# Where the low bits of a 64-bit weight are made, and when the second weight is converted

## The chip, the cores and the metric

One core of one Trainium2 chip runs the whole program. The metric is the time of one execution on the device in microseconds: 1229.4 us, the median of three runs (1228.87 to 1230.52). The program is scheduled when it is built: the order of the instructions on each engine and of the transfers on each queue is fixed then, from priorities and a model of the times; on the chip each engine works through its own list in order and waits at semaphores.

## The reference

```python
# q, k, v: (4, 8, 576, 64); rotary embedding of q and k, then softmax attention
attn = softmax((q_rot @ k_rot.T) / 8)          # 576 x 576 for each of 32 heads
x = (attn @ v), transposed to (2304, 512)
# layer 1: w_in (512, 2048), w_out (2048, 512)
h = x @ w_in;  r = maximum(h, 0);  x = (s * r * r + b) @ w_out
# layer 2: its own w_in (512, 2048), w_out (2048, 512)
h = x @ w_in;  g = h / (1 + exp(-1.702 * h));  out = g @ w_out     # (2304, 512)
```

The four weights arrive as 64-bit floating-point numbers, everything else as 32-bit.

## The kernel before

**Attention** runs over 144 score tiles of 128 queries by 576 keys, 36 for each of four batches (`bounds` is 0, 36, 72, 108, 144). The program is written in *slots*, one for each score tile: `at(slot, fn, ...)` puts a piece of work into a slot, and the slots' pieces are written out in order, each with a priority that falls from slot to slot. For a tile TensorE makes the scores (`score_tile`), VectorE takes the row minimum of the negated scores (L421), ScalarE the exponential (L431), GpSimd scales by the reciprocal sum (L442), and two slots later TensorE transposes the tile (`turn_tile`), ScalarE casts it to 16 bits (L463) and VectorE makes the rest (L465). `weighted` multiplies with the values at the end of each unit of 4 or 5 tiles and stores to `xT`.

**Layer 1** runs beside attention from slot 42 on, in passes over 256 tokens and 16 blocks of its 2048 inner columns. `target` spreads its half blocks evenly over the slots up to 146, so a slot carries the same amount of TensorE work of layer 1 whenever it runs. What is left of it, and layer 2, follow after attention, when `late` is set: attention's pools are closed (`widen`, in the code after the last slot), and new pools take over their space, with the buffers for layer 2's weights (`fill`, L671 and L558) and for x of layer 1's last pass (L791).

**The weights' conversion** from 64 to 32 bits is done on the chip. A 64-bit number is read as two 32-bit words, high and low. ScalarE scales the high word, read as a float, by 2^-112 (L526, L614), which puts the exponent right; VectorE shifts the low word right by 29, so that three bits are left (L528, L615); VectorE then puts the sign into the low word (L531, L616), and shifts the high word left by 3 and joins the low one (L537, L619). `to_f32` does this for 128x512 numbers at a time. Layer 1's 32 such pieces (`weight`) come during attention, 16 in slots 2 to 34 and 16 in slots 36 to 68, by `conv_slot`; the 16 pieces of layer 2's second weight (`outer_make`) come after attention through the same function.

Layer 2's **first weight** goes through `top_load` and `top_max`, 32 pieces of 128x256: a load into the one buffer `top`, the conversion, the piece's largest absolute value (L622) and a store to `w2f` in DRAM. Before, piece i is loaded in slot 40 + 3i and converted in slot 42 + 3i, so from 40 to 135. `top_send` (137) reduces the maxima and sends them through DRAM (`tops`) to all partitions (`wrow`); `top_scale` (141) makes the scales from them. `combine` reads `w2f` and the scales after attention.

`hold` ties an operation behind the row minimum of the newest score tile in its engine's order while attention runs. Nearly all transfers are issued by SyncE, in one order; an issue that has to wait holds up those behind it.

Of the kernel before, what the change touches and what calls it, by code (L numbers as in the profile page):

```python
# [14 lines left out]
AF = mybir.ActivationFunctionType  # L15
ALU = mybir.AluOpType
# [12 lines left out]
def kernel(  # L29
# [14 lines left out]
    nc = tc.nc  # L44
# [41 lines left out]
    def pin(ins, chain="pe"):  # L86
        if chain in chains:
            tc.add_manual_dep(
                ins.ins,
                chains[chain],  # L90
                mybir.DependencyInfo(
                    mybir.DependencyClass.NoSync, mybir.DependencyReason.SCHED_ONLY
                ),
                reason=chain,
            )
        chains[chain] = ins.ins.name
# [9 lines left out]
    def hold(ins):  # L106
        if anchor and not late:
            tc.add_manual_dep(
                ins.ins,
                anchor[-1],  # L110
                mybir.DependencyInfo(
                    mybir.DependencyClass.NoSync, mybir.DependencyReason.SCHED_ONLY
                ),
                reason="hold",
            )
        return ins

    def f32(ap):
        return ap.bitcast(F32)
# [387 lines left out]
    def dv(ins):  # L507
        if late:
            pin(ins, "dve")
        return ins  # L510

    def pace(ins):
        if "dve" in chains:
            tc.add_manual_dep(
                ins.ins,
                chains["dve"],
                mybir.DependencyInfo(
                    mybir.DependencyClass.NoSync, mybir.DependencyReason.SCHED_ONLY
                ),
                reason="pace",  # L520
            )

    def to_f32(raw):
        words = raw.bitcast(U32).rearrange("p (n z) -> p n z", z=2)
        low, high = words[:, :, 0], words[:, :, 1]
        ins = nc.scalar.activation(f32(high), f32(high), AF.Copy, scale=2.0**-112)  # L526
        pace(hold(ins))
        dv(hold(nc.vector.tensor_scalar(low, low, 29, None, op0=ALU.logical_shift_right)))  # L528
        yield 0.55
        dv(  # L530
            nc.vector.scalar_tensor_tensor(  # L531
                low, high, 0x80000000, low, op0=ALU.bitwise_and, op1=ALU.bitwise_or
            )
        )
        yield 0.75
        dv(
            nc.vector.scalar_tensor_tensor(  # L537
                low, high, 3, low, op0=ALU.logical_shift_left, op1=ALU.bitwise_or
            )
        )  # L540
        yield 0.8
        return f32(low), f32(high)
# [29 lines left out]
    def weight(f, m):  # L572
        if f in STREAMED:
            weight_load(f, m)
            t = wpool.tile([128, 2, 512], F32R, tag=f"ws{m}", name=f"w0_{f}{m}")
        elif f == NF - 1:
            t = wpool.tile([128, 2, 512], F32R, tag=f"w10{1 - m}", name=f"w0_{f}{m}")
            kept.setdefault(f, []).append(t)
        elif m == 0:
            t = wpool.tile([128, 4, 512], F32R, tag=f"w{HELD.index(f)}", name=f"w0_{f}")  # L580
            kept[f] = [t[:, 0:2], t[:, 2:4]]
        if f not in STREAMED:
            t = kept[f][m]
        low, high = at_once(to_f32(halves0.pop((f, m))))
        nc.scalar.copy(t[:, 0], low)
        nc.vector.tensor_tensor(t[:, 1], low, f32(t[:, 0]), op=ALU.subtract)
        if f in STREAMED:
            d = dram.tile([128, 2, 512], F32, tag=f"wd{f}{m}", name=f"wd{f}{m}")
            spill[f, m] = d
            at(conv_slot(f, m) + SPILL, lambda: nc.sync.dma_start(d, f32(t)))  # L590
# [18 lines left out]
    def top_max(i):  # L609
        t = wtop.pop(i)  # L610
        words = t.bitcast(U32).rearrange("p (n z) -> p n z", z=2)
        low, high = words[:, :, 0], words[:, :, 1]
        flat = t.bitcast(F32)[:, 0:256]
        hold(nc.scalar.activation(f32(high), f32(high), AF.Copy, scale=2.0**-112))  # L614
        hold(nc.vector.tensor_scalar(low, low, 29, None, op0=ALU.logical_shift_right))  # L615
        nc.vector.scalar_tensor_tensor(  # L616
            low, high, 0x80000000, low, op0=ALU.bitwise_and, op1=ALU.bitwise_or
        )
        nc.vector.scalar_tensor_tensor(  # L619
            flat.bitcast(U32), high, 3, low, op0=ALU.logical_shift_left, op1=ALU.bitwise_or  # L620
        )
        nc.vector.tensor_reduce(  # L622
            wmax[:, i : i + 1], flat, axis=AX.X, op=ALU.max, apply_absolute_value=True
        )
        nc.sync.dma_start(
            w2f.rearrange("(p c) f -> p (c f)", p=128)[:, i * 256 : (i + 1) * 256], flat
        )
# [88 lines left out]
    def outer_make(f, tag):  # L716
        o = late["m2"].tile([128, 2, 512], F32R, tag="g", name=f"wm{f}", bufs=3)
        low, high = yield from to_f32(take())
        pace(nc.scalar.copy(o[:, 0], low))
        dv(nc.vector.tensor_tensor(o[:, 1], low, f32(o[:, 0]), op=ALU.subtract))  # L720
        yield 0.7
        done_with(1)
        nc.sync.dma_start(made[f], f32(o))
# [24 lines left out]
    late = {}  # L748
# [435 lines left out]
    def at(slot, fn, *args):  # L1184
        tasks.setdefault(slot, []).append((fn, args))
# [120 lines left out]
                at(first - 4, value_load, b, p, vts[p])  # L1306
                at(first - 2, value_split, b, p, vts[p])
    for i in range(32):
        at(40 + 3 * i, top_load, i)
        at(42 + 3 * i, top_max, i)  # L1310
    at(137, top_send)
    at(141, top_scale)
    at(3, v_first, 0, first_scale)
    at(4, v_spread, 0, first_scale)
    for f in range(NF):
# [114 lines left out]
```

## Time and profile before

| what | before |
|---|---|
| median of three runs | 1229.4 us |
| the profiled execution's own time | 1225.09 us |
| its span, first to last instruction | 1222.9 us |
| mean granted TensorE clock | 0.965 |
| bytes read from HBM and written to it | 150.24 MB, 51.12 MB |
| attention's last store | issued at 681.5 us |

The profile is one execution. The span is shorter than the execution's time by what lies around the first and the last instruction. Busy time of an engine leaves out its waits and the issuing of transfers. A granted clock of 1 is TensorE's upper level, 2.4 GHz; in the stretches at 0.5 it ran at the lower one, 1.2 GHz, so a mean of 0.95 says that a tenth of the stretch was at the lower one. The stages, by the starts of the score tiles: tiles 0 to 35 from 26 to 172 us, 36 to 41 to 194 us, 42 to 66 to 322 us, and the last one, tile 143, at 669.6 us.

### The profile page before, as it was taken

The numbers are of one execution on the slowest core, as the hardware profiler recorded it, in microseconds if no ns is written. First come the engines' busy times: TensorE is split into PE (matmuls) and PEld (weight loads), VectorE is DVE, ScalarE is ACT, GpSimd is POOL, SyncE is SP. The second block draws the span as 40 slices with busy tenths as digits, with TensorE's granted clock in tenths as the row PEclk, the third lists the DMA queues.
The fourth block names the chain that finished last, engine by engine and source line by source line (L and its number), as shares of the span: only waits on it lengthen the run. The fifth ranks groups of instructions, "written<-read, shape, count | busy, mean of one in ns | idle before, by whom it ended". The sixth has DMA issues, their size and how long they took to land.

```text
span 1222.9 us, 22833 instructions
## 1 busy us (share of the span) xinstructions
PE 1100.4 (90%) x8160; PEld 941.4 (77%) x8160; DVE 864.2 (71%) x2006; ACT 690.7 (56%) x1477; POOL 266.7 (22%) x295
## 2 busy tenths in 40 slices
PE   3675767989999999999999799989999999999997
PEld 2554546888889999999999698767777777777775
DVE  5877787989978797777776376766665655755544
ACT  2775675756655655566665587876343343443443
POOL 4475753346334343411111000000000000000000
PEclk9877787999999999999999999989999999999999
DMA  6687868899978878776652599834011101010010
GB/s 151 207 231 207 252 193 268 255 311 292 307 223 290 261 239 250 231 228 212 211 187 94 197 364 372 309 109 155 3 35 35 38 1 37 18 35 3 1 35 18
DMA packets 147873, 209.95 MB, mean 172 GB/s; under 512 B 33712, under 2 KB 106672, under 8 KB 147760
## 3 DMA queue, kind: packets, MB, share of 16 engines
q1 hardware_dynamic: 146896, 207.90, 53.6%
q8 instruction: 65, 1.06, 0.4%
q10 hardware_dynamic: 864, 0.59, 0.2%
q14 instruction: 48, 0.39, 0.1%
HBM read 150.24 MB, written 51.12 MB: 165 GB/s over the span
## 4 chain that ended last, share of the span: by engine, by line
PE 61%; DVE 18%; DMA 8%; ACT 6%; issue 5%; POOL 1%; SPq 1%; ACTq 0%; DVEq 0%; POOLq 0%
PE acc L99 26%; PE l L99 22%; PE av L99 4%; PE s L99 4%; PE t L99 4%; DVE P L421 3%; DVE pt L465 2%; PE r L102 1%; DMA w2f<-top 1%; DVE stage L531 1%; DMA top<-in_moe_w_in_dram 1%; DVE stage L528 1%; DVE stage L537 1%; DMA stage<-in_moe_w_out_dram 1%; ACT P L431 1%
## 5 line engine op out<-in xcount | busy, mean ns | idle before, releaser
L99 PE MATMUL acc<-wo,g 128*128 128x512 f32 x864 | 248.6, 413 | 1.3 <-ACT g L949 0.7
L99 PE MATMUL l<-xc,wc 128*128 128x256 f16 (+1 forms) x1680 | 199.2, 263 | 0.7 <-DVE c L942 0.7
L442 POOL TENSOR_SCALAR P<-P,st 128x576 f32<-128x576 f32 x144 | 118.2, 821 | 355.6 <-DVE st L441 185.7
L99 PEld LDWEIGHTS <-wc 128*128 128x128 f16 x1680 | 137.6, 98 | 65.9 <-issue 54.1
L99 PE MATMUL acc<-g,w 128*128 128x256 f32 (+1 forms) x1056 | 162.1, 302 | 10.8 <-DVE g L845 9.9
L99 PEld LDWEIGHTS acc<-wo,g 128*128 128x128 f32 x864 | 148.3, 189 | 26.8 <-ACT g L949 2.5
L99 PEld LDWEIGHTS acc<-g,w 128*128 128x128 f32 x1056 | 141.8, 192 | 18.9 <-DVE g L845 12.2
L431 ACT ACTIVATE P<-P,st 128x576 f32<-128x576 f32 x144 | 112.0, 778 | 66.7 <-DVE P L421 66.4
L421 DVE TENSOR_SCALAR_CACHE_REDUCE P<-s 128x576 f32<-128x576 f32 x144 | 108.1, 750 | 41.0 <-PE s L99 39.2
L99 PE MATMUL t<-ident,P 128*128 128x128 f32 x720 | 111.1, 289 | 26.6 <-POOL P L442 8.8
L99 PE MATMUL l<-xh,w 128*128 128x256 f32 x616 | 126.9, 289 | 7.0 <-ACT r L832 3.1
L99 PEld LDWEIGHTS t<-ident,P 128*128 128x128 f32 x720 | 86.5, 149 | 35.4 <-issue 18.0
L465 DVE TENSOR_TENSOR pt<-t,pt 128x640 f16<-128x640 f32 x120 | 98.2, 818 | 19.2 <-ACT pt L463 17.2
L99 PEld LDWEIGHTS l<-xh,w 128*128 128x128 f32 x616 | 102.0, 193 | 8.5 <-ACT r L832 3.4
L463 ACT CAST pt<-t 128x640 f16<-128x640 f32 x144 | 98.7, 685 | 16.6 <-PE t L99 13.3
L947 ACT ACTIVATE r<-c 128x512 f32<-128x512 f32 (+1 forms) x80 | 46.9, 587 | 105.3 <-DVE c L942 105.3
L99 PE MATMUL l<-xl,w 128*128 128x256 f32 x308 | 87.7, 285 | 3.1 <-DVE xl L800 3.1
L99 PE MATMUL s<-k,qb 128*128 128x320 f32 x480 | 85.6, 304 | 3.4 <-DVE pt L465 2.2
L953 DVE TENSOR_TENSOR g<-c,g 128x512 fp32r<-128x512 f32 (+1 forms) x80 | 51.1, 639 | 45.2 <-ACT g L949 45.2
L832 ACT ACTIVATE r<-l 128x256 f32<-128x256 f32 x144 | 53.3, 378 | 45.8 <-PE l L99 38.1
L99 PEld LDWEIGHTS s<-k,qb 128*128 128x128 f32 x480 | 70.8, 189 | 10.6 <-issue 4.0
L942 DVE SCALAR_TENSOR_TENSOR c<-l,xm,u 128x256 f32<-128x256 f32 (+1 forms) x120 | 54.6, 455 | 33.1 <-PE l L99 29.0
(143 smaller groups left out, 1982.2 us busy)
## 6 DMA issues: line engine op xcount, KB each, us to landing
ws<-wd SPq DMA_DIRECT2D x80, 512.0 KB, 5.4
k<-ksp SPq DMA_DIRECT2D x24, 576.0 KB, 6.2
stage<-in_moe_w_in_dram SPq DMA_DIRECT2D x16, 512.0 KB, 5.4
stage<-in_moe_w_out_dram SPq DMA_DIRECT2D x16, 512.0 KB, 6.1
top<-in_moe_w_in_dram SPq DMA_DIRECT2D x32, 256.0 KB, 3.3
rawTrue<-in_moe_w_out_dram SPq DMA_DIRECT2D x16, 512.0 KB, 6.2
wod<-wm SPq DMA_DIRECT2D x16, 512.0 KB, 7.6
wo<-wod SPq DMA_DIRECT2D x16, 512.0 KB, 4.5
```

What stands on the lines that cost most here:

```text
L99: pin(nc.tensor.matmul(*args, **kw))
L102: pin(nc.tensor.transpose(*args))
L421: ins = nc.vector.tensor_scalar(pr, ps[:, 192 : 192 + S], -Q_SCALE, None, op0=ALU.mult, op1=ALU.min, accum_out=st[:, 0:1],)
L431: nc.scalar.activation(pr, pr, AF.Exp, bias=st[:, 0:1], scale=-1.0, accum_out=st[:, 1:2])
L442: pin(nc.gpsimd.tensor_scalar(pr, pr, st[:, 2:3], 1.0, op0=ALU.mult, op1=ALU.mult), "pool")
L463: nc.scalar.copy(hi, pc)
L465: nc.vector.tensor_tensor(lo, pc, hi, op=ALU.subtract)
L528: dv(hold(nc.vector.tensor_scalar(low, low, 29, None, op0=ALU.logical_shift_right)))
L832: nc.scalar.activation(r, ps[:, cols], AF.Relu)
L942: dv(nc.vector.scalar_tensor_tensor(o, ps, d, rest, op0=ALU.mult, op1=ALU.add))
L947: nc.scalar.activation(r, c, AF.Tanh, scale=0.851)
L953: dv(nc.vector.tensor_tensor(g2[:, 1], c, f32(g2[:, 0]), op=ALU.subtract))
```

## The change

There are two edits. First, during attention ScalarE makes the three low bits, as `low` times 0.984375 x 2^-29 less 0.484375, written back as an unsigned number, which the conversion rounds; VectorE's shift stays in `to_f32` for the 16 pieces after attention alone. Second, piece i of layer 2's first weight is loaded in slot 64 + floor(5i/2) and converted two slots later: loads from slot 64 to 141, two and three slots apart in turn, conversions from 66 to 143; `top_send` goes to slot 145 and `top_scale` to 148.

```diff
+    def eighths(low):
+        hold(nc.scalar.activation(low, low, AF.Copy, bias=-0.484375, scale=0.984375 * 2.0**-29))
+
     def to_f32(raw):
...
-        dv(hold(nc.vector.tensor_scalar(low, low, 29, None, op0=ALU.logical_shift_right)))
+        if late:
+            dv(hold(nc.vector.tensor_scalar(low, low, 29, None, op0=ALU.logical_shift_right)))
+        else:
+            eighths(low)
...
     def top_max(i):
...
-        hold(nc.vector.tensor_scalar(low, low, 29, None, op0=ALU.logical_shift_right))
+        eighths(low)
...
     for i in range(32):
-        at(40 + 3 * i, top_load, i)
-        at(42 + 3 * i, top_max, i)
-    at(137, top_send)
-    at(141, top_scale)
+        at(64 + 5 * i // 2, top_load, i)
+        at(64 + 2 + 5 * i // 2, top_max, i)
+    at(64 + 4 + 5 * 31 // 2, top_send)
+    at(64 + 7 + 5 * 31 // 2, top_scale)
```

## Rows read from the trace of the kernel before

**Rows 1.** The page: busy us, share of the span and instructions of each engine.
```profile
PE 1100.4 (90%) x8160; PEld 941.4 (77%) x8160; DVE 864.2 (71%) x2006; ACT 690.7 (56%) x1477; POOL 266.7 (22%) x295
```
**Rows 2.** Busy time by stretch: us, each engine's busy us (count), clock, DMA share, GB/s.
```profile
26.00:172.00 146.00, 100.27 (x653) 77.50 (x654) 116.44 (x280) 99.05 (x202) 89.26 (x91) 0.80 0.73 210
172.00:194.00 22.00, 13.53 (x90) 9.80 (x88) 15.70 (x43) 14.22 (x30) 4.30 (x7) 0.84 0.87 271
194.00:322.00 128.00, 113.34 (x964) 107.12 (x965) 118.06 (x278) 83.66 (x179) 54.57 (x52) 0.95 0.88 284
322.00:461.00 139.00, 132.28 (x1167) 125.86 (x1166) 115.97 (x290) 82.88 (x187) 56.66 (x62) 1.00 0.82 259
461.00:633.00 172.00, 168.68 (x1498) 163.41 (x1497) 128.96 (x340) 106.91 (x236) 42.88 (x53) 1.00 0.73 229
633.00:681.00 48.00, 46.31 (x414) 43.68 (x412) 28.94 (x79) 23.86 (x52) 6.74 (x9) 1.00 0.27 97
681.00:702.00 21.00, 14.33 (x109) 13.33 (x109) 7.83 (x18) 14.11 (x31) 0.00 (x0) 1.00 0.69 232
```
**Rows 3.** The same of line L421 alone, two records a score tile.
```profile
194.00:322.00 128.00, 18.22 (x49) 0.95 0.88 284
322.00:461.00 139.00, 22.51 (x60) 1.00 0.82 259
461.00:633.00 172.00, 29.69 (x78) 1.00 0.73 229
```
**Rows 4.** The same of tile top: VectorE's and ScalarE's part.
```profile
194.00:322.00 128.00, 14.80 (x32) 3.60 (x8) 0.95 0.88 284
322.00:461.00 139.00, 17.34 (x40) 4.38 (x10) 1.00 0.82 259
461.00:633.00 172.00, 20.81 (x52) 5.82 (x14) 1.00 0.73 229
```
**Rows 5.** The same of line L528, the shift of layer 1's conversion.
```profile
26.00:172.00 146.00, 10.14 (x16) 0.80 0.73 210
172.00:194.00 22.00, 1.43 (x3) 0.84 0.87 271
194.00:322.00 128.00, 6.14 (x12) 0.95 0.88 284
```
**Rows 6.** Tile stage: duration ns min/median/max, first and last start us, shapes.
```profile
L526 ACT ACTIVATE stage<-stage x32: 654/676/721, 44.9 to 320.2; 128x512 f32<-128x512 f32 x32
```
**Rows 7.** Chain of waits by line, 26 to 172 us.
```profile
by line: issue 13.3%; DVE P L421 8.3%; PE av L99 8.3%; PE s L99 5.9%; PE r L102 5.6%; DVE stage L531 5.0%; POOL nat L285 4.8%; DMA stage<-in_moe_w_out_dram 4.3%; DVE stage L528 4.1%; DVE stage L537 3.9%; PE t L99 3.8%; POOL nat L282 3.1%; D
```
**Rows 8.** Tile top, the same columns.
```profile
L614 ACT ACTIVATE top<-top x32: 422/439/466, 194.2 to 632.9; 128x256 f32<-128x256 f32 x32
L615 DVE TENSOR_SCALAR top<-top x32: 272/295/1474, 194.6 to 634.1; 128x256 uint32<-128x256 uint32 x32
L616 DVE SCALAR_TENSOR_TENSOR top<-top x32: 394/423/1244, 197.7 to 634.7; 128x256 uint32<-128x256 uint32 x32
```
**Rows 9.** Line L606, loads of top: from issue to landing.
```profile
DMA to landing us min/median/max: 2.6/3.3/7.3
```
**Rows 10.** Line L625, stores of top: from issue to landing.
```profile
DMA to landing us min/median/max: 1.7/3.7/8.3
```
**Rows 11.** ScalarE's waits, 322 to 633 us: us in total, times, longest.
```profile
ACT top L614 <- DMA top<-in_moe_w_in_dram: 17.3, 6, 4.3
```
**Rows 12.** SyncE's queue, waits of 190 to 690 us, the same columns.
```profile
SPq L606 <- DMA w2f<-top: 61.0, 24, 6.1
...
SPq L671 <- DMA xT<-pt: 3.7, 1, 3.7
```
**Rows 13.** Timeline of SyncE, 635 to 646 us: start us, us.
```profile
636.89 0.32 SPq L630 DMA_DIRECT2D tops<-wscale  x1
644.30 0.32 SPq L631 DMA_DIRECT2D wrow<-tops  x1
```
**Rows 14.** Timeline of SyncE, 681 to 688 us.
```profile
685.66 0.37 SPq L671 DMA_DIRECT2D rawFalse<-w2f  x1
```

## The prediction, made before the result was known

> **What bounds the kernel now.** I read the totals first, then the engines by stretch, then the pace of the score tiles, then the waits. TensorE is busy 90% of the span and VectorE 71% [rows 1], but these are averages over stages with different limits, so the windows decide [rows 2]. From 322 us until the end of attention at 681 us TensorE is the bound: 132.28 of 139 us, 168.68 of 172, 46.31 of 48, all at full clock, while VectorE falls from 83% to 60%. From 194 to 322 us it is another stage: TensorE 113.34 of 128 us (14.7 us idle) at a granted clock of 0.95, and VectorE 118.06 of 128, 92%. There VectorE is the busiest engine, because this stretch carries the second half of layer 1's weight conversion, the first conversions of layer 2's weight and layer 1's own work together. From 26 to 172 us nothing is full: VectorE 80%, ScalarE 68%, TensorE 69% at a clock of 0.80. The pace says the same: each score tile leaves two records at L421, so 49, 60 and 78 records [rows 3] are 24.5 tiles in 128 us (5.22 us each), 30 in 139 (4.63) and 39 in 172 (4.41). A tile carries the same share of layer 1 from slot 42 on, so the first of these stretches loses some 0.6 us a tile to something else than TensorE's work.
>
> **The change part by part.** The sum is made on the profiled execution, 1225.1 us (span 1222.9); the median of the three runs is 1229.4, so 4.3 us are added at the end.
>
> *A, 194 to 322 us (slots 42 to 66).* Eight conversions of layer 2's weight leave, with 14.80 us of VectorE and 3.60 of ScalarE [rows 4] and their loads and stores; conversion 0 now comes at slot 66. Twelve shifts of layer 1's conversion leave VectorE too: 6.14 us [rows 5]. VectorE then has 118.06 - 14.80 - 6.14 = 97.1 us of work. ScalarE gets twelve operations. The trace has none with uint32 on ScalarE; the nearest row is the Copy of the same 128x512 strided half, 0.676 us [rows 6]. Ends: the shift's own 0.42 us if integers were quicker, twice 0.676 if they took two passes; I take 0.676, since tile and strides are the same. ScalarE: 83.66 - 3.60 + 12 x 0.676 = 88.2 us, no bound. At the busy shares of the next stretch (TensorE 0.952, VectorE 0.834) the work would take 113.3 / 0.952 = 119.1 us by TensorE and 97.1 / 0.834 = 116.4 by VectorE. The longer one holds: 8.9 us less, and about 1 us for the part of the low clock level that goes with the idle time. I take -10. Ends: 0, if the stage hangs on transfers (DMA share 0.88) or on latencies, and -21, which is both all the VectorE time taken out (20.9) and all that TensorE idles (14.7) or loses to the clock (0.05 x 128 = 6.4).
>
> *B, 26 to 194 us (slots 0 to 42).* 16 + 3 shifts leave VectorE, 10.14 + 1.43 us [rows 5]; 19 x 0.676 = 12.8 us come to ScalarE, which goes from 113 to 126 of 168. No engine is full, so only what lies on the chain counts: the chain of waits has the shift with 4.1% of 146 us, 6.0 us [rows 7]. Against it, the first combining operation (L531), which waited for one ScalarE operation, now waits for two: up to 16 x 0.676 = 10.8 us if nothing covers it. Behind it in VectorE's queue stand the score minima (L421), for which ScalarE's Exp waits. The cover is VectorE's other work, 80% of the stretch. Ends -7.4 (6.0 and all of the 1.43) and +4.8 (10.8 - 6.0); I take -2.5, near the middle, leaning to the gain because VectorE is the busier of the two.
>
> *C, 322 to 681 us (slots 66 to 143).* Here stood 24 conversions, three slots apart; now all 32 stand here, two and three slots apart in turn. VectorE: about 41 us before (17.34 for ten, 20.81 for thirteen, [rows 4], and one more at 1.6); after, 32 at about 1.66 - 0.30 (the shift, [rows 8]) = 43 us: no difference. ScalarE gains 32 x 2 x 0.439 - 24 x 0.439 = 17.6 us over 359, from 60 to 64%. TensorE hides both. What isn't hidden for sure is the ring: there is one buffer, so load i+1 waits for the landing of store i, and a conversion waits for its load. At the medians, load 3.3, two ScalarE operations 0.88, two VectorE operations 0.85, store 3.7 [rows 8 to 10] make 8.7 us. Two slots at 4.41 are 8.8 us, 2.5 slots 11.0: it just fits, and landings reach 7.3 and 8.3 us. When it doesn't fit, ScalarE stands in front of the late load with the next tile's Exp, relu and cast behind it. Even at three slots ScalarE waited so 6 times, 17.3 us [rows 11], and SyncE 61.0 us for stores with all other loads behind it [rows 12]. TensorE idled 10.0 us in the same 311 us [rows 2], at most 0.58 of ScalarE's wait. If half of the 16 two-slot rounds wait 2.9 us (17.3 / 6), that is 23.2 us, 5.9 more than now, and 0.58 of it is +3.4. I take +3; ends -1 (the waits don't grow) and +17 (worked out under the rivals).
>
> The Trainium skill (DMA: Bandwidth & Descriptors, on the fixed cost of a transfer) gives a transfer about 2.0 us of setup and completion. By that a round would be an estimated 2.0 + 0.88 + 0.85 + 2.0 = 5.7 us, the ring would never wait, and C would be 0 and the sum 3 us lower. The landings here, 3.3 and 3.7 us at the median beside a DMA share of 0.73 to 0.82, are longer, and I go by them.
>
> *D, the end of attention.* The last load moves from slot 133 to 141, the maximum's way through DRAM from 137 to 145, the scales from 141 to 148, after the last tile (143). Before, nothing waited for them: `tops` was issued at 636.89 and `wrow`, when that had landed, at 644.30 [rows 13]. Now the last conversion comes beside tile 143, some 35 us later than beside tile 135 (8 tiles at 4.41): `tops` near 672 on the old clock, `wrow` near 679.5, landed 3.7 to 8.3 us later by the stores' row [rows 10], at 683 to 688, and then reduced. The late buffers take over attention's space, and their first load (L671) waited 3.7 us for attention's last store to land [rows 12] and went out at 685.66 [rows 14]. As far as that wait covers all of attention's tiles, it now ends where it did or, with both transfers slow, near 690. Behind it on SyncE stand the loads of x for layer 1's last pass. TensorE has little left to cover it: 14.33 of 21 us busy from 681 to 702 [rows 2]. I take +1, ends 0 and +5. The last four conversions add 5.4 us of VectorE to a stretch where it is busy 28.94 of 48: hidden.
>
> Sum: -10 - 2.5 + 3 + 1 = -8.5; 1225.1 - 8.5 = 1216.6 us, and 1220.9 on the scale of the median.
>
> **The rivals.**
> 1. *The stage isn't VectorE's.* For it: DMA share 0.88, and VectorE's 92% holds operations stretched beyond their quiet length (6.14 us for twelve shifts of 0.42). Against it: TensorE's share rises exactly where VectorE's falls. Then A is -3 or less, B nothing, C and D stay: 1225.1 - 3 + 3 + 1, about 1230 on the median's scale.
> 2. *The ring sets the pace (slower).* Place: ScalarE and SyncE between slots 66 and 143. All 16 two-slot rounds wait 2.9 us, 46.4 us in place of 17.3; at 0.58 of it TensorE loses 17. It decides from the point where a round lasts more than 8.8 us at the median, 0.1 above my figure. For it: the medians leave nothing over, and the added ScalarE operation lengthens each round. Against: waits of 3 to 4 us late in the stage left no TensorE idle time worth the name (3.3 us in 461 to 633). Sum -10 - 2.5 + 17 + 1 = +5.5: 1234.9.
> 3. *More is freed than counted.* With idle time gone the clock stays at its full level through slots 36 to 66, and the first stretch loses the whole shift: A -15, B -6, C +1, D +1: -19, 1210.4.
> That the conversion isn't moved at all can't be: no data sets the order.
>
> **How the numbers follow.** A difference under 0.2% (2.5 us) can't be told from no change here, so faster begins below 1226.9. Forecast 0.57 (A between -6 and -14: 1216 to 1226), rival 1 0.15, rival 2 0.18, rival 3 0.10. Faster: the forecast, rival 3 and a little of rival 1, 0.70. Same: the rest of rival 1 and the mildest of rival 2, 0.12 and 0.01. Slower: the rest of rival 2, 0.17. For 8 in 10 the range takes the forecast, most of rival 3 and rival 1 and all but the far side of rival 2: 1209 to 1235; the forecast's own range is 1216 to 1226.
>
> **What would show it.** Right: in the stretch from tile 42 to tile 66 TensorE's share rises to about 0.95 and the time falls from 128 to about 118 us; VectorE's busy time there falls to about 97; the 32 early shifts are gone and ScalarE has 32 new operations of about 0.68 us and 32 of about 0.44; the pace of tiles after 66 stays within 0.05 us of 4.63 and 4.41. C is wrong if ScalarE's wait for `top` loads passes 40 us and TensorE's idle time after tile 66 grows by over 8 us. D is wrong if the first late load goes out more than 5 us after attention's last store has landed. The whole prediction is wrong if the stretch from tile 42 to 66 keeps its 5.2 us a tile with VectorE at 80%.

## The result and the profile after

The change makes the kernel slower: 1238.35 us, median of four runs (1236.55 to 1242.82), against 1229.13 (1228.64 to 1230.52) before, a ratio of 1.0074 with a 95% interval of 1.0046 to 1.0103. The forecast was 1220.9, the range 1209 to 1235. The profiled execution took 1236.55 us (before 1225.09), its span is 1234.7 (1222.9).

The engines' totals answer to [rows 1] (PE is TensorE, PEld its weight loads, DVE VectorE, ACT ScalarE, POOL GpSimd, SPq SyncE's queue of transfers):

```profile
PE 1104.6 (89%) x8160; PEld 945.1 (77%) x8160; DVE 848.6 (69%) x1942; ACT 715.0 (58%) x1541; POOL 266.2 (22%) x295
```

VectorE has 64 instructions fewer and ScalarE 64 more, as the diff says. The new operations, tile by tile (duration ns min/median/max, first and last start):

```profile
L524 ACT ACTIVATE stage<-stage x32: 649/661/702, 45.8 to 322.4; 128x512 uint32<-128x512 uint32 x32
...
L524 ACT ACTIVATE top<-top x32: 412/426/448, 321.5 to 671.0; 128x256 uint32<-128x256 uint32 x32
```

They cost what the prediction took from the float Copy beside them (0.676 and 0.439, [rows 6, 8]). The stretches, cut at the starts of the same score tiles as in [rows 2], with attention's end cut once more (us, then the busy time of PE, PEld, DVE, ACT and POOL, granted clock, DMA share, GB/s):

```profile
26.00:174.00 148.00, 99.68 (x653) 76.60 (x654) 116.54 (x264) 107.44 (x219) 92.90 (x91) 0.83 0.76 208
174.00:196.00 22.00, 13.67 (x89) 10.56 (x88) 14.54 (x38) 14.87 (x31) 3.15 (x5) 0.80 0.85 259
196.00:322.50 126.50, 114.25 (x967) 107.87 (x966) 103.90 (x235) 87.11 (x186) 51.47 (x52) 0.93 0.82 265
322.50:460.00 137.50, 132.17 (x1172) 126.45 (x1171) 113.05 (x285) 87.21 (x202) 56.62 (x62) 1.00 0.84 266
460.00:635.00 175.00, 169.07 (x1492) 162.90 (x1492) 128.94 (x335) 111.80 (x253) 43.01 (x53) 1.00 0.72 228
635.00:681.00 46.00, 44.55 (x390) 42.24 (x389) 29.56 (x78) 26.37 (x59) 6.73 (x9) 1.00 0.52 123
681.00:694.00 13.00, 3.62 (x25) 2.67 (x24) 2.13 (x9) 0.41 (x1) 0.00 (x0) 0.63 0.33 67
```

Two things are to be seen. From 196 to 322.5 us, tiles 42 to 66, VectorE's busy time fell from 118.06 to 103.90 us, but the stretch only from 128 to 126.5: the gain that was forecast there did not come. And from 681 to 694 TensorE works 3.62 of 13 us, a hole that the kernel before does not have (14.33 of 21 from 681 to 702). Tile 143 starts at 671.7 us, 2.2 after before; the loads of x go out 10.6 after, of the 11.8 us by which the span grew. So most of the loss in this pair of traces lies in the last 26 us of attention. The timeline there (start, duration, engine, line, in brackets the idle time ahead of it and what ended it):

```profile
674.38 0.81 DVE L465 TENSOR_TENSOR pt<-t,pt 128x640 f16<-128x640 f32 x1
...
674.49 0.32 SPq L636 DMA_DIRECT2D tops<-wscale  x1
...
677.77 0.82 DVE L465 TENSOR_TENSOR pt<-t,pt 128x640 f16<-128x640 f32 x1 [0.31 <-ACT pt L463]
...
682.89 0.32 SPq L637 DMA_DIRECT2D wrow<-tops  x1
...
687.64 0.28 DVE L640 TENSOR_REDUCE wscale<-wrow 128x1 f32<-128x128 f32 x1 [9.05 <-DMA wrow<-tops]
687.85 0.47 DVE L844 SCALAR_TENSOR_TENSOR g<-r,sb,g 128x256 fp32r<-128x256 f32 x1
...
689.06 0.81 DVE L465 TENSOR_TENSOR pt<-t,pt 128x640 f16<-128x640 f32 x1
689.93 3.62 PE L99 MATMUL av<-pt,vf 128*64 128x320 f16 x25 [9.21 <-DVE pt L465]
...
694.14 0.32 SPq L501 DMA_DIRECT2D xT<-pt  x1
...
696.28 0.37 SPq L677 DMA_DIRECT2D rawFalse<-w2f  x1
...
697.72 0.98 SPq L797 DMA_DIRECT2D x<-xT  x2
```

VectorE's list has the reduction of `wrow` (L640) in front of the last tile's rest (L465). `wrow` lands only at 687.6, so VectorE stands for 9.05 us, and with it TensorE, which needs that rest for attention's last product. Those 25 matmuls then take 3.62 us, partly at the lower clock level, where the kernel before has:

```profile
678.95 1.93 PE L99 MATMUL av<-pt,vf 128*64 128x320 f16 x25 [0.40 <-DVE pt L465]
```

The first late load (L677) answers to [rows 14]: 696.28 against 685.66.

The ring's waits answer to [rows 11, 12]. ScalarE's for loads of `top`, 322 to 635 us (us in total, times, longest):

```profile
ACT top L620 <- DMA top<-in_moe_w_in_dram: 22.3, 10, 3.4
```

SyncE's for the store ahead of the next load, 322 to 640 us, in the same columns:

```profile
SPq L612 <- DMA w2f<-top: 49.1, 23, 5.6
```

A new wait stands behind the first, in VectorE's list from 322.5 to 635 us: VectorE no longer waits for the load itself (9.4 us in 5 waits before, 322 to 670 us) but for ScalarE's low bits.

```profile
DVE top L622 <- ACT top L524: 19.1, 13, 2.7
```

### The profile page after: what moved, and what is told of

Read it like the earlier page. It is cut to its first block, busy times and chain, and to the rows that moved or that the text cites. A ratio compares the mean times of both kernels' runs of the same rounds, so it can differ in the third digit from the quotient of the medians.

```text
span 1234.7 us, 22816 instructions
## 1 busy us (share of the span) xinstructions
PE 1104.6 (89%) x8160; PEld 945.1 (77%) x8160; DVE 848.6 (69%) x1942; ACT 715.0 (58%) x1541; POOL 266.2 (22%) x295
## 4 chain that ended last, share of the span: by engine, by line
PE 60%; DMA 14%; DVE 12%; ACT 6%; issue 4%; POOL 2%; SPq 1%; DVEq 0%; ACTq 0%; POOLq 0%
PE acc L99 26%; PE l L99 23%; PE s L99 4%; PE av L99 4%; PE t L99 3%; DMA top<-in_moe_w_in_dram 3%; DVE P L421 2%; DMA w2f<-top 2%; DMA stage<-in_moe_w_in_dram 1%; DVE pt L465 1%; ACT P L431 1%; DMA nat<-in_k_dram 1%; PE r L102 1%; DMA qb<-qsp 1%; DVE wc L704 1%
## 5 line engine op out<-in xcount | busy, mean ns | idle before, releaser
L99 PE MATMUL acc<-g,w 128*128 128x256 f32 (+1 forms) x1056 | 162.9, 303 | 11.3 <-DVE g L851 10.6
L99 PEld LDWEIGHTS acc<-wo,g 128*128 128x128 f32 x864 | 148.3, 189 | 26.8 <-ACT g L955 2.5
L421 DVE TENSOR_SCALAR_CACHE_REDUCE P<-s 128x576 f32<-128x576 f32 x144 | 108.0, 750 | 44.7 <-PE s L99 38.0
L465 DVE TENSOR_TENSOR pt<-t,pt 128x640 f16<-128x640 f32 x120 | 98.2, 819 | 16.7 <-ACT pt L463 14.8
L102 PE MATMUL r<-ident,nat 128*128 128x128 f32 (+1 forms) x160 | 35.1, 327 | 49.4 <-DVE z L307 16.7
```

What stands on the lines that cost most here:

```text
L99: pin(nc.tensor.matmul(*args, **kw))
L102: pin(nc.tensor.transpose(*args))
L421: ins = nc.vector.tensor_scalar(pr, ps[:, 192 : 192 + S], -Q_SCALE, None, op0=ALU.mult, op1=ALU.min, accum_out=st[:, 0:1],)
L465: nc.vector.tensor_tensor(lo, pc, hi, op=ALU.subtract)
```

## The experiments

Ratios are to the kernel before, run on the same chip, with 95% intervals. "66 to 143" is the time between the starts of these tiles, "tail" that from the start of tile 143 to the first late load, both of one profiled execution.

| kernel | median us | ratio | 66 to 143 | tail |
|---|---|---|---|---|
| before | 1229.13 | 1 | 347.8 | 16.1 |
| the change | 1238.35 | 1.0074 [1.0046, 1.0103] | 349.3 | 24.5 |
| tail tied | 1234.8 | 1.0040 [1.0018, 1.0063] | 351.0 | 17.9 |
| slots only | 1243.1 | 1.0097 [1.0065, 1.0129] | 359.4 | 24.7 |
| low bits only | 1231.28 | 0.9994 [0.9974, 1.0014] | 354.0 | 15.8 |
| start 56 | 1253.47 | 1.0178 [1.0148, 1.0208] | 367.1 | 15.9 |
| three slots from 48 | 1228.77 | 0.9976 [0.9955, 0.9996] | 341.7 | 19.4 |
| conversion one slot later | 1241.62 | 1.0103 [1.0068, 1.0139] | 357.6 | 18.1 |
| start 60 | 1251.83 | 1.0167 [1.0146, 1.0189] | 371.7 | 14.1 |
| shorter round | 1230.99 | 0.9999 [0.9980, 1.0018] | 346.0 | 18.5 |
| late tail on before | 1229.88 | 0.9995 [0.9976, 1.0015] | 349.9 | 13.8 |
| three slots from 44 | 1230.58 | 1.0011 [0.9988, 1.0034] | 344.6 | 16.1 |
| three slots from 46 | 1229.45 | 0.9989 [0.9971, 1.0007] | 351.2 | 15.5 |
| own store buffer, 64 | 1229.82 | 1.0004 [0.9985, 1.0022] | 345.9 | 18.9 |
| own store buffer, 60 | 1229.88 | 0.9996 [0.9973, 1.0019] | 347.8 | 13.9 |
| own store buffer, 48 | 1231.51 | 1.0027 [1.0007, 1.0047] | 346.2 | 18.7 |

On one chip 29 runs of the kernel before spread from 1223.9 to 1237.6 us, so a difference of a few us between two single profiles proves nothing; the profiled execution of the store buffer from 64, for one, is the fastest of its twelve (1222.61). The verdicts below go by ratios and by waits that can be pointed at. By the traces TensorE runs the same 8160 operations in the same order in all sixteen kernels; what differs is the lists of the other engines and of the transfers.

**1. The tail tied.** The reduction of `wrow` is put behind the last tile's rest in VectorE's list; only these rows of VectorE's list change places, no other engine's list does.

```diff
-            nc.vector.tensor_tensor(lo, pc, hi, op=ALU.subtract)
+            last_rest.append(nc.vector.tensor_tensor(lo, pc, hi, op=ALU.subtract).ins.name)
...
     def top_scale():
-        up, neg, down = (wscale[:, i : i + 1] for i in range(3))
+        up, neg, down, _ = (*(wscale[:, i : i + 1] for i in range(3)), anchor.append(last_rest[-1]))
```

> The changed kernel with one edge more in the build: the reduction of `wrow` (L640) is put behind the last tile's rest (L465) on VectorE; nothing else moves on any engine. Theory T (VectorE waits 9.0 us for `wrow` in front of the last tile's L465 and L844, and that is the loss): about 9 us faster than the changed kernel, 1229 to 1232 us, and TensorE's gap of 9.2 us before the last av gone. Rival R (the denser ring of loads and stores between slots 66 and 143 costs the time, the wait at the end only shows it): 1236 us or more. Rival W (the late buffers wait for `wrow` all the same, so its reduction is late wherever it stands): about half comes back, 1233 to 1236.

VectorE now finishes the last tile first, and waits for `wrow` with nothing behind it:

```profile
682.52 0.82 DVE L465 TENSOR_TENSOR pt<-t,pt 128x640 f16<-128x640 f32 x1 [1.25 <-ACT pt L463]
...
683.40 1.93 PE L99 MATMUL av<-pt,vf 128*64 128x320 f16 x25 [0.40 <-DVE pt L465]
...
684.85 0.32 SPq L637 DMA_DIRECT2D wrow<-tops  x1
...
690.08 0.29 DVE L640 TENSOR_REDUCE wscale<-wrow 128x1 f32<-128x128 f32 x1 [6.74 <-DMA wrow<-tops]
...
691.90 0.37 SPq L677 DMA_DIRECT2D rawFalse<-w2f  x1
```

The tail goes from 24.5 to 17.9 us: 6.7 of the 8.5 us that the change added come back. The other 1.8 are not the wait for the scales, which were done at 691.32. The first late load went out when attention's last store had landed, at 691.72:

```profile
SPq L677 <- DMA xT<-pt: 5.5, 1, 5.5
```

That store took 5.8 us to land, 4.0 before; the scales alone would have held the load only 0.4 us less. By the medians the step is smaller, from 1.0074 to 1.0040, some 4 us, with intervals that meet. What is left, 0.4% or 5 us, is for the most part not the tail.

**2 and 3. Each half of the change alone.** One has the later slots and VectorE's shift, the other the slots of before and ScalarE's low bits.

The first, against the change (in both conversions):

```diff
-        eighths(low)
+        hold(nc.vector.tensor_scalar(low, low, 29, None, op0=ALU.logical_shift_right))
```

> The later slots alone: the low three bits stay VectorE's shift everywhere. T: the wait for `wrow` is there as in the changed kernel, 1236 to 1241 us. R: also slow, 1236 to 1241, with the time lost between tiles 66 and 143. My sum's part A, if right, shows in tiles 42 to 66: 14.8 us of VectorE gone, 128 us falls to about 121.

The second, with `top_max`, `top_send` and `top_scale` back at 42 + 3i, 137 and 141:

```diff
-        at(64 + 5 * i // 2, top_load, i)
+        at(40 + 3 * i, top_load, i)
```

> ScalarE's three bits alone: loads and conversions of layer 2's weight stay in slots 40 to 135. T: no wait at the end, 1227 to 1231 us. My sum: part of A (6.1 us of VectorE) and B, -2.5 to -6, so 1223 to 1227. A rival, that the added ScalarE operation lengthens each conversion and nothing else was bound by VectorE: 1230 to 1233.

The low bits on ScalarE change nothing clear of noise (0.9994), and the slots alone cost as much as the whole change (1.0097 against 1.0074; the intervals overlap). So the loss belongs to the slots. Tiles 42 to 66 took 121.3 us with the slots alone, as I had expected from part A, and 123.9 with the low bits alone; VectorE was busy for 106.7 and 108.8 us there, and for 103.9 in the change, which took 126.0. So VectorE's load there does not decide. What the slots alone won there went again behind it: tiles 66 to 143 took 359.4 us, 11.6 more than before.

**4. Start at 56.**

```diff
-        at(64 + 5 * i // 2, top_load, i)
-        at(64 + 2 + 5 * i // 2, top_max, i)
-    at(64 + 4 + 5 * 31 // 2, top_send)
-    at(64 + 7 + 5 * 31 // 2, top_scale)
+        at(56 + 5 * i // 2, top_load, i)
+        at(56 + 2 + 5 * i // 2, top_max, i)
+    at(56 + 4 + 5 * 31 // 2, top_send)
+    at(56 + 7 + 5 * 31 // 2, top_scale)
```

> The changed kernel with 56 in place of 64: the same density of the ring (two and three slots apart) and the same ScalarE operation, eight slots earlier, so the last conversion stands in slot 135 and `wrow` is back long before the last tile. T: the loss at the end is gone, 1226 to 1231 us. R: the ring is as dense, so 1236 or more stays.

The tail was cured (15.9 us), but tiles 66 to 143 took 19 us longer than before. Rival R, the dense ring, had said 1236 or more; my theory had not seen it coming. The next four runs ask why.

**5. Three slots a round, from 48**, with the tie and ScalarE's low bits.

```diff
-        at(64 + 5 * i // 2, top_load, i)
-        at(64 + 2 + 5 * i // 2, top_max, i)
+        at(48 + 3 * i, top_load, i)
+        at(50 + 3 * i, top_max, i)
```

> The first experiment (after, with wrow's reduction tied behind the last tile) with one thing more changed: piece i of layer 2's first weight is loaded in slot 48 + 3i and converted in slot 50 + 3i, so every round of the ring has three slots as before the change, and the last conversion stays at slot 143. Theory (the 2.5-slot ring costs about 6 us between tiles 84 and 120): those 36 tiles take 162 us, as before the change (161.7; 168.2 in the first experiment); the gain of tiles 66 to 84 (82.3 against 85.4) goes away as conversions spread; total 1229 to 1233. Rival (any move of the slots reshuffles the order of loads and of TensorE's work, and density is not what costs): tiles 84 to 120 stay at 166 us or more, total 1234 to 1240. A third view, from the run that began at slot 56: conversions of both weights together between slots 48 and 68 cost by themselves; then tiles 48 to 68 lose 3 us or more against before.

Tiles 84 to 120 took 161.4 us, as the ring's theory said (before 161.7), though tiles 66 to 84 kept their gain, which it had not said. Tiles 48 to 68 took 104.3 us against 101.6, a little under the 3 us of the third view. The total, 0.9976, lies just under no change.

**6. Layer 1's conversion one slot later.**

```diff
-    CONV = 2
+    CONV = 3
```

> The first experiment (after, with the tie) with the late conversions of layer 1's weight three slots behind their loads instead of two. Theory A' (tiles 42 to 66 are held by loads of the stage tile that land late, not by an engine): TensorE's idle time there falls from 9.8 us to under 6 and the stretch from 124.6 to 121 us or less; total 1230 to 1232. Rival (the idle time comes from the start of layer 1 and from single late transfers of weights and keys, and the rest is TensorE's own work, partly at the lower clock level): the stretch stays within 2 us of 124.6, total 1233 to 1237.

Tiles 42 to 66 took 125.6 us, so late loads of `stage` do not hold them. The total, 1.0103, was missed by both; that layer 1's conversion now reaches further into the slots of the ring may be the reason, but no run takes that apart.

**7. Start at 60**, with the tie.

> The first experiment (after, with the tie) with 60 in place of 64, so loads from slot 60 to 137, the last conversion at 139, wrow reduced near tile 141. The tail: first late load within 16.5 us of tile 143's start, as before the change. Theory (what cost 26 us in the run from slot 56 is the dense ring beside layer 1's conversion, which lasts until slot 68: 12 slots there, 4 after the change, 8 here): tiles 54 to 120 lose about half of that, total 1240 to 1246. Rival (slot 56 met an unlucky order of transfers and TensorE's work, and the overlap alone is harmless): attention as in the first experiment, total 1231 to 1235.

Both missed: the tail is short, as expected, but the kernel lost as much as from slot 56. The trace shows how. One round of the ring in it:

```profile
481.09 0.53 SPq L631 DMA_DIRECT2D w2f<-top  x1
...
488.40 0.34 SPq L612 DMA_DIRECT2D top<-in_moe_w_in_dram  x1
...
491.19 0.43 ACT L620 ACTIVATE top<-top 128x256 f32<-128x256 f32 x1 [5.78 <-DMA top<-in_moe_w_in_dram]
491.53 0.41 ACT L524 ACTIVATE top<-top 128x256 uint32<-128x256 uint32 x1
...
491.97 0.43 DVE L622 SCALAR_TENSOR_TENSOR top<-top 128x256 uint32<-128x256 uint32 x1 [6.03 <-ACT top L524]
...
494.28 1.30 PE L99 MATMUL t<-ident,P 128*128 128x128 f32 x5 [4.06 <-DVE pt L465]
```

Piece i's store goes out at 481.09 and lands 7.3 us later; only then does the load of piece i + 1 go out, at 488.40. ScalarE has that conversion next in its list and stands 5.78 us, VectorE stands 6.03 behind ScalarE, and TensorE 4.06 behind VectorE's rest of a tile that has nothing to do with the ring. In the microseconds after it the granted clock falls as well:

```profile
486.00:490.00 4.00, 4.00 (x35) 4.00 (x33) 0.00 (x0) 0.00 (x0) 0.00 (x0) 1.00 0.60 191
490.00:494.20 4.20, 0.22 (x2) 0.01 (x1) 2.19 (x7) 2.36 (x6) 0.62 (x1) 0.93 0.87 275
494.20:498.00 3.80, 3.72 (x23) 3.58 (x25) 2.53 (x7) 2.15 (x5) 0.88 (x2) 0.63 0.78 211
498.00:502.00 4.00, 4.00 (x46) 3.50 (x43) 1.74 (x4) 1.70 (x4) 0.00 (x0) 1.00 0.27 68
```

**8. A shorter round.** The conversion of `top` keeps the scaling and the joining, and leaves out the low bits and the sign:

```diff
-        eighths(low)
         nc.vector.scalar_tensor_tensor(
-            low, high, 0x80000000, low, op0=ALU.bitwise_and, op1=ALU.bitwise_or
-        )
-        nc.vector.scalar_tensor_tensor(
-            flat.bitcast(U32), high, 3, low, op0=ALU.logical_shift_left, op1=ALU.bitwise_or
+            flat.bitcast(U32), high, 3, low, op0=ALU.logical_shift_left, op1=ALU.bitwise_and
         )
```

> The first experiment (after, with the tie) with less work in each piece of layer 2's first weight: the low three bits and the sign are left out (one ScalarE operation of 0.43 us and one VectorE operation of 0.42 us less, and a handing over between the two engines); loads, scaling, joining, maximum and store stay, so the ring's transfers are the same and its round is about 1 us shorter. The result of layer 2 is not the reference's. Theory (the ring's round decides between tiles 84 and 120): these tiles fall from 168.2 to 163 us or less, ScalarE's wait for top loads falls to under 12 us, total 1228 to 1231. Rival (the transfers' density or the order decides, not the round): tiles 84 to 120 stay at 166 us or more, total 1233 to 1236.

The total came back to 0.9999, by about 4 us, as the ring's theory said. Its path was off: tiles 84 to 120 fell to 165.9 us, not under 163, and ScalarE's wait did not fall at all (26.8 us; 21.1 with the tie alone). This pointed to the ring without showing it.

**9. The late tail alone on the kernel before.**

```diff
-    at(137, top_send)
-    at(141, top_scale)
+    at(145, top_send)
+    at(148, top_scale)
```

> The kernel before with one thing alone: top_send in slot 145 (before 137) and top_scale in slot 148 (before 141), as in the change; the slots of the 32 pieces and VectorE's shift stay. The data of the last piece are there eight tiles earlier than in the change. Theory D' (what the tail costs is set by the order that the build writes for VectorE: the reduction of wrow ahead of tile 143's rest, with a round trip through DRAM of 7 to 8 us that the build counts as short): up to tile 143 nothing changes; VectorE stops for 6 us or more at the reduction, the first late load goes out 22 us or more after tile 143's start (before 16.1, with the change 24.6), total 6 to 9 us over before. Rival (the tail is late because the last conversions are late): the first late load within 18 us of tile 143's start, total within 2.5 us of before.

My theory failed here. The reduction stands ahead of the last three tiles' rests in VectorE's list, and nothing waits:

```profile
675.11 0.28 DVE L634 TENSOR_REDUCE wscale<-wrow 128x1 f32<-128x128 f32 x1
...
677.04 0.82 DVE L465 TENSOR_TENSOR pt<-t,pt 128x640 f16<-128x640 f32 x1
```

`tops` still went out at 641.75, long before slot 145, since its data were there and the build had written it where it could run. So the stall needs both: the last conversion at tile 143, which puts `tops` at 674.49, and the order. Experiment 1 took the one away, this one the other.

**10 and 11. Three slots a round, from 44 and from 46.**

> The run with pieces in slots 48 + 3i, moved four slots earlier: load in 44 + 3i, conversion in 46 + 3i (the last in 139), top_send in 141, top_scale in 144; ScalarE makes the low bits, the tie stays. Theory (the late buffers wait for wrow's reduction, 3.3 us more than before in the run from slot 48; three-slot rounds cost nothing): first late load within 17 us of tile 143's start, attention as in the run from slot 48 to within 2 us, total 1225 to 1228 beside a before of 1231, faster by 0.25 to 0.45%. Rival (each move of the slots reshuffles the order and costs or gains some us by chance): attention 3 us or more longer than in the run from slot 48, total 1229 to 1238, although the tail is as short.

> The same with load in 46 + 3i, conversion in 48 + 3i (the last in 141), top_send in 143, top_scale in 146. Theory: first late load 16 to 19 us after tile 143's start, between the runs from slots 44 and 48; total 1226 to 1229. Rival (chance of the order): attention 3 us or more longer than in the run from slot 48, total 1230 to 1238.

The tails are short, 16.1 and 15.5 us, and no time is won: 1.0011 and 0.9989. Attention was longer, as the rival said (3 us or more): tile 143 starts 9.6 and 2.9 us later than in the run from slot 48. The 0.9976 from there is not borne out by its neighbours.

**12 to 14. A buffer of its own for the store**, so that a load waits for the joining operation and no longer for the store to land; slots from 64, from 60 and (three a round) from 48, all with the tie. One column tile is shared with another to make room.

```diff
-        flat = t.bitcast(F32)[:, 0:256]
+        flat = att.tile([128, 256], F32, tag="flat", name=f"flat{i}", bufs=1)
```

> The first experiment (after, with the tie; loads from slot 64, 2.5 slots apart) with a buffer of its own for the converted piece, from which the store goes: the next load waits for the joining operation only, and no longer for the store's landing. Everything else stays. Theory (the ring's round, load, conversion and store one after the other, decides after tile 66): SyncE's wait of 56.7 us before top loads falls under 15, ScalarE's wait for top (21 us) under 8, tiles 66 to 143 take 344 us or less (first experiment 351.0, before 347.8), total 1224 to 1228 beside a before of 1229 to 1231. Rival (what differs between the versions is the order that the build writes, by chance, not the ring): tiles 66 to 143 stay at 348 us or more, total 1230 to 1236.

> The run from slot 60 (1251.8 us, tiles 66 to 143 371.7 us, ScalarE waiting 48.9 us for top) with the buffer of its own for the converted piece. Theory (ring): tiles 66 to 143 fall to 350 us or less, ScalarE's wait for top under 12, total 1224 to 1232. Rival (order or overlap with layer 1's conversion): tiles 66 to 143 stay over 360 us, total 1240 or more.

> The run from slot 48 with three slots a round (1228.8 us) with the buffer of its own for the converted piece. Theory (ring): a round of three slots mostly had room, ScalarE waited 10.5 us; that falls under 4, tiles 66 to 143 go from 341.7 us to 339 to 342, total 1226 to 1229, a gain of 0 to 0.4% over before. Rival (order by chance): 3 us or more to either side of 341.7.

The run from slot 60 settles what the ring costs there. The same slots go from 1251.83 to 1229.88 us, 1.0167 to 0.9996. Tiles 66 to 143 from slot 60 with the one buffer (the columns as above, us from the span's start):

```profile
325.00:697.00 372.00, 345.52 (x2994) 331.89 (x2994) 268.75 (x686) 220.04 (x502) 105.42 (x123) 0.98 0.70 218
```

and with the store's own buffer:

```profile
323.00:672.00 349.00, 338.81 (x2999) 327.05 (x2999) 268.40 (x686) 222.99 (x504) 103.94 (x124) 1.00 0.74 232
```

The engines' counts are the same to five; TensorE's idle time falls from 26.5 to 10.2 us, and its busy time from 345.5 to 338.8, since the clock is at its lower level for 3.4 us of this stretch and no longer for 17.1. 23 us are the ring. That the build wrote another order by chance is hardly left as a rival: TensorE's and GpSimd's lists are the same in both, and in VectorE's and ScalarE's some 40 of 1240 and 20 of 940 entries change places, the ring's own among them. The wait of SyncE for the store is gone (66.6 us before, no longer in the list), and the waits for `top` are halved; ScalarE's is still 21.7 us in this stretch, where I had expected under 12. What ended the idle time ahead of operations on `top`, us and times, from slot 60 with one buffer:

```profile
  DMA top<-in_moe_w_in_dram: 48.9, 19
  ACT top L524: 36.6, 16
```

and with two:

```profile
  DMA top<-in_moe_w_in_dram: 23.9, 12
  ACT top L525: 14.9, 10
```

From slot 64 the step is 1.0040 to 1.0004, some 4 us, with intervals that just meet, and ScalarE's wait goes from 21.1 to 8.1 us. Tiles 84 to 120 show the step best, with the tie alone and then with the store's own buffer (columns as above):

```profile
405.30:573.60 168.30, 162.29 (x1422) 155.65 (x1422) 125.75 (x328) 103.11 (x238) 54.92 (x64) 0.99 0.76 236
402.30:563.80 161.50, 159.28 (x1419) 153.68 (x1418) 128.85 (x327) 103.98 (x238) 55.03 (x64) 1.00 0.79 246
```

These tiles take 161.4 to 161.7 us in the kernel before and in five of the six other versions with three slots a round (164.5 with the late tail alone), and 165.9 to 179.1 in the seven with two and a half slots and one buffer. So in these tiles some 5 us of the change are the ring. SyncE's wait ahead of the loads fell only to 29.4 us, now for the joining operation, and tiles 66 to 143 took 345.9 us, between the theory's 344 and the rival's 348. The gain over before that I expected (1224 to 1228) is not there. From slot 48, where the ring had room, nothing is won either (1.0027), and tiles 66 to 143 take 4.5 us more, as the rival of chance had it.

No version clearly beats the kernel before. Those in which the ring and the tail cost little (no tail is more than 3.3 us over before) lie between 0.9976 and 1.0027 in no order that I can explain; another order of the build may be worth that much here, which no run takes apart.

## Why the prediction was wrong

**A, the step that failed most** ("At the busy shares of the next stretch (TensorE 0.952, VectorE 0.834) the work would take 119.1 us"). The change took 14 us of VectorE's busy time out of tiles 42 to 66 and the stretch gave back 2. Not even VectorE's part of the sum came out (97.1 forecast, 103.9 measured): [rows 4, 5] count their operations by themselves, but VectorE's operations overlap, and their single durations in these tiles add up to 137.0 us where it is busy for 118.0. The main fault is the step from VectorE's load to the time. The mean over 128 us hid two different halves. The kernel before:

```profile
194.00:262.00 68.00, 56.00 (x461) 52.85 (x462) 59.18 (x133) 42.51 (x91) 29.84 (x30) 0.90 0.89 285
262.00:322.00 60.00, 57.34 (x505) 54.27 (x504) 58.88 (x146) 41.15 (x88) 24.73 (x22) 1.00 0.88 282
```

and after the change:

```profile
196.00:264.00 68.00, 56.88 (x466) 53.80 (x465) 51.47 (x112) 44.16 (x94) 31.32 (x30) 0.87 0.85 276
264.00:322.50 58.50, 57.37 (x503) 54.07 (x503) 52.43 (x124) 42.95 (x92) 20.14 (x22) 1.00 0.80 253
```

In the first half TensorE idles 12 us and runs part of the time at the lower level; VectorE has 59.18 of 68, and with 51.47 the half lasts as long. TensorE waits there for single things. Its longest waits from 196 to 322.5 us after the change are one weight transfer (2.0 us before, 1.4 with the slots alone, none with the low bits alone) and the first x of layer 1 (us in total, times, longest):

```profile
PE l L99 <- DMA ws<-wd: 4.8, 1, 4.8
PE l L99 <- DVE xl L806: 2.4, 1, 2.4
```

In the second half VectorE is at 98% in the kernel before, and TensorE idles only 2.7 of 60 us: VectorE was full and just kept up, and there were 2.7 us to win, not 10. The rows for this could have been read beforehand by cutting the stretch once. Rival 1 named the right side (A small, B nothing). The sign that I had named for the whole prediction being wrong is there too: 5.27 us a tile (126.5 for 24) with VectorE at 82%. Why the slots alone took only 121.3 us here stays open; 5.5 of the 6.6 us won lie in tiles 42 to 54, the first half.

**B** was put at -2.5 between -7.4 and +4.8. With the low bits alone there was no change clear of noise (0.9994, from 3.2 us less to 1.7 more), so the total does not rule out 2.5 us. The stretch speaks against a gain: tiles 0 to 42 took 167.3 to 176.1 us in the thirteen kernels with layer 1's low bits on ScalarE, with a median of 172.1, and 167.9, 168.8 and 170.1 in the three without. The shift did leave the chain of waits, 4.3% of 168 us before; the ScalarE operation did not take its place (0.6 us with the low bits alone). What did stays open.

**C** had the right mechanism and about the right price: +3 forecast, some 4 us taken back by the second buffer from slot 64. The bound of +17 was too near for other starts: from slots 60 and 56 the same ring cost 20 us and more; why it costs so much more from there than from 64 no run shows. The remark against rival 2, that waits of 3 to 4 us had left no idle time, did not hold for longer ones: the wait of 5.78 us shown above, with VectorE behind ScalarE, stopped TensorE for 4.06. The signs that I had named were too coarse: ScalarE's wait stayed under 40 us, and the idle time after tile 66 grew by about 1 us only, since 3.5 us gained in tiles 66 to 84 hide some 5 lost in tiles 84 to 120. (The "about 41 us" of VectorE was 39.8: 17.34 + 20.81 + 1.6. Nothing hangs on it.)

The Trainium skill (DMA: Bandwidth & Descriptors, on the fixed cost of a transfer) gives about 2.0 us, by which the ring would never wait; its fit is for transfers that GpSimd issues, and adds the time of the bytes (an estimated 0.6 us for 256 KB at its 436 GB/s). The trace differs: the stores' landings have a median of 4.3 us and reach 8.1 in the run from slot 60.

**D** failed in one clause: "As far as that wait covers all of attention's tiles, it now ends where it did or, with both transfers slow, near 690." The times were right (`tops` forecast near 672, measured 674.49; `wrow` near 679.5, measured 682.89; landed at 683 to 688, measured 687.6). What was wrong is who waits first. I followed the late buffers and never asked where the reduction of `wrow` stands in VectorE's list. It stood ahead of attention's last rest. +1 forecast, ends 0 and +5; the tail grew by 8.5 us in the profile, and tying it gave back 6.7 there and some 4 by the medians. The sign for D stayed silent, since the stall held up attention's last store too: the first late load went out 0.2 us after that had landed.

Put together: 12.5 us of A and B that did not come, about 1 more for the ring and 3 to 7 more for the tail make up, as far as they can be told apart, the 17 us between 1220.9 and 1238.35.

## What to carry to other kernels

Before counting on an engine that looks full, cut its stretch until the halves agree: here an engine at 98% beside a TensorE that idles 4% was no bound, and what could be won was TensorE's idle time there, not the work taken out. For work that is moved late, list what its engine has in order behind each wait it brings, since here the first to wait was a neighbour with nothing to do with it. In a ring of one buffer count load, work and the store's landing at its slow end, not its median, and give the store a buffer of its own before spacing the ring closer.

## What the hardware showed unexpectedly

- A column of 4 bytes a partition is slow on its way to DRAM, next to 3.7 us at the median for the stores of 128x256 words [rows 10]. From issue to landing, transfers of L636 (`tops` and others through the same line) after the change:

```profile
DMA to landing us min/median/max: 7.3/7.7/8.9
```

The way back to all partitions (L637) takes 4.7 us at the median. The Trainium skill (DMA: Bandwidth & Descriptors, Specifications) says that transfers under 512 bytes read, modify and write; whether that is the cause no run here shows.
- ScalarE converts 128x512 strided uint32 words as fast as it copies floats of the same layout (0.661 and 0.678 us).
- A stop of TensorE of 4.06 us amid full work was followed by some 3.4 us at the lower clock level (0.63 over 3.8 us, above); from slot 60 such spells after tile 66 cost about 7 us beyond the stops themselves. The length of one stop does not tell: in the same run two stops of 2.0 us (at 358.6 and 439.5 us) were followed by such a spell and two of 2.2 and 2.3 us (393.9 and 539.6) were not, nor was one of 2.3 us at 353.4 us in the kernel before.
